# Sparse attention feeding a softplus feed-forward layer: a condition on the strided visits, and a new order for the first chunk

## The chip, the core and the metric

The kernel runs on one core of a Trainium2 chip. Its time is device microseconds of that core. Each core has five engines that run side by side, each through its own list of instructions in order: TensorE (PE, with its weight loads shown as PEld), VectorE (DVE), ScalarE (ACT), GpSimd (POOL) and SyncE (SP), which here issues nearly all DMA transfers. Matmuls write to PSUM, from which ACT and DVE copy results into SBUF.

## What is computed

```python
def attention(q, k, v):                        # 8 batches, 8 heads, 576 positions, 64 wide
    scores = q @ k^T / sqrt(64)
    rel = pos[:, None] - pos[None, :]
    local   = (rel >= 0) & (rel < 32)                       # heads 0 to 3
    strided = (rel >= 0) & (pos[:, None] % 32 == pos[None, :] % 32)   # heads 4 to 7
    scores = where(mask, scores, -1e9)
    return softmax(scores) @ v

x = attention(...)                              # 4608 tokens x 512
h = x @ w_in                                    # 512 -> 2048
g = max(h, 0) + log1p(exp(-|h|))                # softplus
out = g @ w_out                                 # 2048 -> 512
```

All inputs and outputs are float32. For the feed-forward layer the kernel splits every operand into a high and a low part in a format that PE multiplies quickly, and adds three products (high by high, high by low, low by high).

## The kernel before

**Attention.** Two heads make a pair; a batch has two local pairs (0, 1) and two strided ones (2, 3), taken in the order 0, 2, 1, 3, so that the 32 pairs are numbered n = 0 to 31 and every odd n is strided. Pairs 0 to 3 (the first batch) are worked through before the feed-forward layer starts; each later pair n has a *visit* (`visit`, L832), a bundle of small matmuls on PE between two steps of the feed-forward layer. A strided visit first forms the weighted sums of the pair before it (`late_weighted`, L451; its matmuls are L475 or, for a strided pair, L461), then its own scores (`late_scores`, L410; L422 for strided pairs). The strided scores go into two PSUM buffers of the pool `ps_h`, which has just two and is shared with the hidden steps (tile name `ph`). DVE then adds the mask (`add_mask`, L533), and a row softmax follows on DVE and ACT, with DVE transposes at its end (L580 for strided pairs, L592 for local ones).

**Feed-forward layer.** The 4608 tokens are nine chunks of 512, and the 2048 hidden columns sixteen blocks of 128. Step i = 16 x chunk + block. Its hidden part F (`hidden`, L720; twelve matmuls, L729) fills a `ph` buffer. ACT then takes Abs, Exp and Ln (L741, L744, L746), DVE forms the softplus u (`softplus`, L748; the instruction is L750), which sets the `ph` buffer free, and its high and low part. Two steps later the output part O (`output`, L764; twelve matmuls, L769, three for each of four tiles of 128 tokens) adds to the four accumulators `py`. At a chunk's end the `py` banks are copied out (`result`, tile `o`) and stored.

**What sets the order.** Two lists. The first chunk, with the attention of pairs 0 to 8, follows a table of names that is written out by hand (`FIRST`): k, q, v, wi, wo are loads; S scores, X maxima, E exponents, R and M normalization, T transposes, C copies out of PSUM, V weighted sums, H and L the high and low part of x; a, B, d, h, l the conversion of weights; F, A, u, Gh, Gl, O the feed-forward steps; J visits; W filler matmuls. `ON_POOL`, `ON_VECTOR` and `ON_SCALAR` name the steps that leave their usual engine, `WIDE` the two score blocks whose exponents are one wide instruction (after a subtraction on DVE) instead of one for each of their groups. Everything later goes through a planner (`Plan`, L96): each task has an urgency, an engine, a cost and a list of tasks that it stands behind; the planner places them one by one into the first gap of their engine and emits them in the order of planned start. This order becomes the order of each engine's instructions; the waits between engines come from the data. The planner's costs only sort, they don't wait.

A visit S of pair n stands at step i (L1006 to L1009) behind the queries and keys that it needs, the transposes of the pair before, and the softplus of step i - 1. It does not stand behind its own step's softplus u{i}, nor behind the output part O{i-2} that shares its place.

Of the kernel before, what the change touches and what calls it, by code (L numbers as in the profile page):

```python
# [40 lines left out]


FIRST = """
mask k0 q0 wi0 W q1 S01 ai0 X01 k1 S00 wo0 x01 X00 S11 x00 q2 W19 S10 k2 k3 E01 Bi0 q3 E00 X11 di0
ao0 v0 X10 hi0 r0 wi9 x10 R0 M0 S20 T02 Bo0 do0 C02 x11 v1 T00 T01 v2 S21 E10 wi1 X20 li0 E11 C01
C00 S30 ho0 V00 r1 Y20 X21 wi3 R1 x21 E20 S31 v3 V02 E21 Z20 wi2 M1 T11 X30 V01 X31 Y30 H00 q4 r2
C11 R2 L00 lo0 x31 T12 E30 M2 T10 H01 k4 Z30 L01 ai9 C12 E31 V11 T20 C10 Bi9 V12 wo6 V10 r3 T22 C20
H10 di9 T21 R3 L10 wo1 H11 wi4 C22 wo2 L11 M3 V22 C21 ai1 V20 V21 H20 Bi1 di1 T32 hi1 C32 H21 T31
wo3 ai3 L20 C31 L21 Bi3 T30 C30 V32 ai2 di3 li1 V31 V30 H30 H31 hi3 Bi2 wi6 L30 D4 L31 Fa0 di2 wi8
wo4 hi9 ao6 J4 Y42 Y40 v4 hi2 F0 li3 li2 W18 wi10 wi5 ao1 A0 Bo1 Y41 Ae0 Fa1 Al0 wi7 ai4 do1 q5 wo15  # L50
li9 Bo6 F1 wo8 u0 wi13 Gh0 ho1 Km A1 wo10 Bi4 lo1 Ae1 ao3 F2 Gl0 di4 wo5 Al1 hi4 O0 A2 do6 X4 u1 ho6
F3 lo6 ai6 Bi6 Gh1 li4 ao2 Ae2 s4 wo13 Bo2 Al2 Gl1 ai8 di6 Bo3 Bi8 do3 E4 u2 hi6 Z4 r4 do2 k5 ho3
di8 R4 li6 O1 Gh2 A3 Ae3 Al3 M4 F4 u3 Gl2 wi11 P41 ho2 lo2 Gh3 Gl3 F6 O2 A4 wi14 ai5 Ae4 wi12 P40
Al4 lo3 ai7 A6 hi8 P42 Bi5 ao4 Bi7 Kz di5 D5 u4 hi5 Ae6 P43 O3 Al6 u6 Gh4 Gh6 J5 v5 k7 di7 li8 li5
Bo4 ai11 ao5 Y51 wo14 Y50 F5 X5 H40 Gl4 wo7 hi7 Bi11 k6 do4 A5 s5 ho4 E5 Bo5 lo4 li7 Ae5 F9 Z5 ai10
wo11 r5 Al5 wo12 Gl6 di11 R5 wo9 q6 A9 Ae9 Bi10 O4 u5 ao8 di10 M5 do5 Gh5 Al9 hi11 hi10 u9 Gl5 F7
ho5 P53 A7 lo5 F8 H41 Bo8 L40 Ae7 Gh9 P51 ao7 Gl9 wi15 Al7 D6 O5 li10 A8 P50 do8 u7 P52 Ae8 ai12 O6
L41 ho8 Al8 Bo7 J6 u8 li11 v6 F10 Gh7 ai13 Y60 do7 Gh8 H51 Y61 lo8 Gl8 ho7 q7 Y62 X6 Bi12 lo7 H50
Gl7 F11 ao9 A10 di12 s6 ao10 Ae10 hi12 Bi13 Al10 Bo10 di13 u10 A11 O7 li12 E6 ai14 L50 hi13 F12 Z6
r6 Bo9 Ae11 do9 ho9 Bi14 R6 M6 Al11 do10 L51 li13 u11 D7 lo9 O8 Gh11 ho10 F13 ao13 Gh10 P60 Gl11 A12  # L60
O9 P62 di14 P63 Gl10 k8 hi14 Ae12 li14 P61 ao11 A13 Al12 lo10 u12 Ae13 Al13 Gh12 ao12 u13 ai15 Bo11
do11 J7 Bo12 Y71 do12 H61 Y70 O10 X7 Gh13 H60 v7 Gl12 Bo13 ho11 lo11 W23 s7 do13 E7 ho12 Bi15 F14 Z7
r7 A14 lo12 di15 R7 hi15 L61 L60 M7 ao15 li15 Ae14 q8 ho13 D8 P72 Al14 k9 P71 Gl13 lo13 P70 u14 O11
O12 F15 Bo15 A15 O13 P73 Ae15 Al15 J8 Gh14 u15 ao14 Bo14 H70 do14 H71 L71 L70 Qa0 Gl14 q9 Gh15 Q0
do15 ho15 QA0 ho14 lo14 O14 Gl15 Qu0 Q1 lo15 QA1 Ob15 O15 y1 Qu1 Qh0 y2 Qh1 y0 v8 y3 Ql0 Ql1
"""

ON_POOL = """
x00 hi0 r0 x10 x11 x21 x31 r3 hi1 hi9 ho1 hi4 hi8 hi7 r5 hi10 ho5 Gh7 hi13 r6 hi14 ho11 r7 Gh14 ho14
""".split()  # L70
ON_VECTOR = """
M0 C02 li0 C11 C12 C10 C21 C32 li1 hi3 li2 lo1 Gl0 lo6 Gl1 Gl2 Gl4 lo4 Gl6 lo7 Gl7 Gl12 lo12 hi15 D8
Gh15 ho15
""".split()
ON_SCALAR = """
y1 y3
""".split()

WIDE = """
20 30  # L80
""".split()


class Plan:
# [8 lines left out]
    def add(self, name, urgency, engine, cost, fn, after=(), late=0.0):  # L93
        self.tasks[name] = (urgency, len(self.tasks), engine, cost, fn, after, late)

    def run(self):  # L96
        busy, end, start = {}, {}, {}

        def place(name):
            if name in end:  # L100
                return
            _, _, engine, cost, _, after, late = self.tasks[name]
            after = [a for a in after if a in self.tasks]
            for a in after:
                place(a)
            t = max([end[a] + self.WAIT for a in after], default=0.0)
            spans = busy.setdefault(engine, [])
            for x, y in spans:
                if y > t:
                    if x - t >= cost:  # L110
                        break
                    t = y
            spans.append((t, t + cost))
            spans.sort()
            start[name], end[name] = t, t + cost + late

        for name in sorted(self.tasks, key=lambda n: self.tasks[n][:2]):
            place(name)
        for name in sorted(self.tasks, key=lambda n: (start[n], self.tasks[n][1])):
            self.tasks[name][4]()  # L120
# [3 lines left out]
def attention_softplus_ffn(  # L124
# [10 lines left out]
    B, NPAIR, _, _, S = qk.shape  # L135
# [95 lines left out]
    def is_local(n):  # L231
        return order[n][1] < NPAIR // 2
# [38 lines left out]
    def lay_out_q(n, engine=nc.scalar):  # L271

        to = qT[:, :S].rearrange("p (m l) -> p m l", l=32)
        copy_on(engine, to, raws[n].rearrange("p (l m) -> p m l", l=32))
# [535 lines left out]
    LAG = 2  # L810
# [124 lines left out]
    t = 0.0  # L935
# [16 lines left out]
    def visited(i):  # L952
        return when[i] + (2.72 if pushes(i) else 0)

    for i in range(begin, len(steps) + LAG):
        if i < len(steps):
            c, f = steps[i]
            x = when[i]
            after = [f"F{i-1}", f"u{i-2}"] + wanted.get(c, [])
# [173 lines left out]
```

## Time and profile before

| | |
|---|---|
| median of 3 runs | 878.86 us (878.12 to 880.0) |
| the profiled execution | 880.72 us |
| its span, first to last instruction | 878.9 us |
| PE busy | 863.3 us, 98% |
| DVE busy | 590.4 us, 67% |
| ACT busy | 395.5 us, 45% |
| mean granted TensorE clock | 0.998 |

A row of an engine's instructions reads: start, duration, engine, source line, operation, output tile <- input tiles, shapes, how often in a row; in brackets the idle time of the engine ahead of it and what ended it. A row of the list of waits reads: who waited <- for whom: total us, times, longest. A row by stretches gives for each engine its busy time and, in brackets, its number of instructions, then the granted TensorE clock, the share of DMA and GB/s. Matmuls overlap, so each row of PE is longer than its share of the stream; what counts is the distance between starts.

### The profile page before, as it was taken

To read this page: it belongs to the slowest core of one execution; us is meant where nothing else is said; L and a number is where in the kernel's file an instruction comes from. 1 tells how busy PE (TensorE), PEld (TensorE's weight loads), DVE (VectorE), ACT (ScalarE), POOL (GpSimd) and SP (SyncE) were. 2 spreads that over 40 slices of the span, in tenths; PEclk is the share of its full clock that TensorE was granted. 3 is DMA by queue.
4 is the path that set the end of the run, shared out by engine and by line. 5 is a ranking of instruction groups with operands and counts; after the bars stand their busy time and mean duration, and the time that the engine had idled before them with its cause. 6 is when DMAs were issued, how large, how long until landed. Compare 5 with 4: busy or idle time off the path is not lost.

```text
span 878.9 us, 16412 instructions
## 1 busy us (share of the span) xinstructions
PE 863.3 (98%) x6704; PEld 706.5 (80%) x6704; DVE 590.4 (67%) x1282; ACT 395.5 (45%) x703; POOL 75.4 (9%) x97
## 2 busy tenths in 40 slices
PE   7999999999999999999999999999999999999998
PEld 4788888888788878888788878888788888888886
DVE  5999968777876777768685867677776533333332
ACT  5877735444444443443444444344443333333332
POOL 4566650000000000000000000000000000000000
PEclk9999999999999999999999999999999999999999
DMA  9975103111210121102211121012100010001001
GB/s 305 345 274 188 48 14 103 49 50 43 90 42 22 49 75 42 43 28 56 76 43 42 43 90 43 15 47 85 41 16 16 1 48 1 1 1 48 1 1 48
DMA packets 46465, 56.46 MB, mean 64 GB/s; under 512 B 3322, under 2 KB 31670, under 8 KB 46390
## 3 DMA queue, kind: packets, MB, share of 16 engines
q1 hardware_dynamic: 46102, 55.09, 19.5%
q8 instruction: 52, 0.85, 0.4%
q10 hardware_dynamic: 288, 0.33, 0.2%
q14 instruction: 23, 0.19, 0.1%
HBM read 45.97 MB, written 9.44 MB: 63 GB/s over the span
## 4 chain that ended last, share of the span: by engine, by line
PE 95%; ACT 2%; DVE 2%; issue 1%; DMA 1%; SPq 0%; POOL 0%; DVEq 0%; ACTq 0%
PE ph L729 45%; PE py L769 44%; PE ps L422 1%; PE ps L461 1%; PE ps L443 1%; PE ps L475 1%; DMA early_h<-in_qk_dram 1%; DVE u L750 1%; ACT u L744 1%; ACT u L746 1%; ACT u L741 0%; PE pv L622 0%; PE py L393 0%; PE po L443 0%; PE po L461 0%
## 5 line engine op out<-in xcount | busy, mean ns | idle before, releaser
L769 PE MATMUL py<-w_o,gh 128*128 128x512 f32 x1152 | 357.8, 392 | 0.0
L729 PE MATMUL ph<-x_h,w_i 128*128 128x512 f32 x1152 | 355.6, 390 | 1.0 <-DVE prob L533 0.5
L741 ACT ACTIVATE u<-ph 128x512 f32<-128x512 f32 x144 | 86.1, 598 | 376.0 <-PE ph L729 375.7
L729 PEld LDWEIGHTS ph<-x_h,w_i 128*128 128x128 f32 x1152 | 215.6, 188 | 47.0 <-DVE u L750 1.1
L769 PEld LDWEIGHTS py<-w_o,gh 128*128 128x128 f32 x1152 | 214.3, 188 | 44.8
L769 PE MATMUL py<-w_o,gl 128*128 128x512 f32 x576 | 224.2, 389 | 0.0
L729 PE MATMUL ph<-x_l,w_i 128*128 128x512 f32 x576 | 224.1, 389 | 0.0
L750 DVE SCALAR_TENSOR_TENSOR u<-ph,u 128x512 f32<-128x512 f32 x144 | 99.2, 689 | 181.6 <-ACT u L746 180.1
L769 PEld LDWEIGHTS py<-w_o,gl 128*128 128x128 f32 x576 | 108.1, 188 | 22.7
L729 PEld LDWEIGHTS ph<-x_l,w_i 128*128 128x128 f32 x576 | 108.1, 188 | 22.6
L762 DVE TENSOR_TENSOR gl<-u,gh 128x512 fp32r<-128x512 f32 x135 | 93.4, 692 | 10.9 <-PE po L475 0.5
L746 ACT ACTIVATE u<-u 128x512 f32<-128x512 f32 x144 | 91.0, 632 | 4.3
L744 ACT ACTIVATE u<-u 128x512 f32<-128x512 f32 x144 | 91.0, 632 | 4.3
L592 DVE STREAM_TRANSPOSE masks_pt<-prob 32x160 f32<-32x160 f32 x224 | 70.1, 317 | 3.9
L269 DVE CAST gh<-u 128x512 fp32r<-128x512 f32 x129 | 54.6, 424 | 8.6 <-PE py L769 0.5
L580 DVE STREAM_TRANSPOSE pt_groups<-prob 32x192 f32<-32x192 f32 (+1 forms) x112 | 39.6, 354 | 3.1
L580 DVE STREAM_TRANSPOSE masks_pt<-prob 32x160 f32<-32x160 f32 (+1 forms) x112 | 39.6, 354 | 3.1
L548 ACT ACTIVATE prob<-prob 128x576 f32<-128x576 f32 (+1 forms) x28 | 19.4, 693 | 46.2 <-DVE prob L542 46.2
L269 ACT COPY qT<-prob 128x576 f32<-128x576 f32 x27 | 34.5, 1279 | 6.0 <-PE ps L422 5.2
L552 DVE TENSOR_REDUCE st<-prob 128x9 f32<-128x576 f32 (+1 forms) x28 | 21.2, 758 | 9.2 <-ACT prob L548 9.2
L533 DVE TENSOR_TENSOR prob<-ps,masks_pt 128x320 f32<-128x320 f32 (+1 forms) x28 | 10.8, 390 | 24.6 <-PE ps L443 14.5
L269 DVE COPY o<-py 128x512 f32<-128x512 f32 (+1 forms) x16 | 10.7, 670 | 16.9 <-PE py L769 16.9
(105 smaller groups left out, 587.1 us busy)
## 6 DMA issues: line engine op xcount, KB each, us to landing
out_dram<-o SPq DMA_DIRECT2D x35, 256.0 KB, 2.0
ri<-in_moe_w_in_dram SPq DMA_DIRECT2D x16, 512.0 KB, 9.8
ro<-in_moe_w_out_dram SPq DMA_DIRECT2D x16, 512.0 KB, 6.8
prob<-in_qk_dram SPq DMA_DIRECT2D x28, 288.0 KB, 2.8
kT<-in_qk_dram SPq DMA_DIRECT2D x28, 288.0 KB, 3.4
v_in<-in_v_dram SPq DMA_DIRECT2D x14, 162.0 KB
v_in<-in_v_dram SPq DMA_DIRECT2D x14, 160.0 KB, 3.1
v_in<-in_v_dram SPq DMA_DIRECT2D x14, 128.0 KB, 3.1
```

The costliest lines, as they stand in the source:

```text
L269: (engine.copy if engine is nc.scalar else engine.tensor_copy)(dst, src)
L548: nc.scalar.activation(pv, pv, AF.Exp, scale=SCALE)
L552: nc.vector.tensor_reduce(sm, pv, axis=AX.X, op=ALU.add)
L580: nc.vector.transpose(dst[:, :, :32], src[:, :, :32])
L592: nc.vector.transpose(pt_late[lo : lo + 32, h, windows, col : col + 32], src[:, :, 32 * c : 32 * c + 32],)
L729: nc.tensor.matmul(ph, lhsT=w32["i", f][:, half, cc * P : (cc + 1) * P], rhs=x_of(x, cc)[:, t0 : t0 + n], start=(i == 0), stop=(i == 3 * N ...
L741: nc.scalar.activation(us[c, f], phs[c, f], AF.Abs)
L744: nc.scalar.activation(u, u, AF.Exp, scale=-1.0)
L746: nc.scalar.activation(u, u, AF.Ln, bias=1.0)
L750: nc.vector.scalar_tensor_tensor(u, in0=phs.pop((c, f)), scalar=0.0, in1=u, op0=ALU.max, op1=ALU.add)
L762: engine.tensor_tensor(g, us.pop((c, f)), ghs[c, f].bitcast(F32), op=ALU.subtract)
L769: nc.tensor.matmul(py[t], lhsT=g[:, sl], rhs=w32["o", f][:, half], start=(f == 0 and n == 0), stop=(f == NFC - 1 and n == 2),)
```

## The change

Two things change. In the later list a strided visit gets two more tasks that it stands behind: the whole output part of its place, O{i-2}, and its own step's softplus u{i}, the latter with a lead of 0.7 us, by which the planner may place the visit ahead of the softplus' end (a name in the list may now be a pair of a name and a lead). In the first list the names stand in another order, with some steps on other engines and another block among the wide ones.

```diff
@@ FIRST, ON_POOL, ON_VECTOR, WIDE: the tables are replaced; for example
-mask k0 q0 wi0 W q1 S01 ai0 X01 k1 S00 wo0 x01 X00 S11 x00 q2 W19 S10 k2 k3 E01 Bi0 q3 E00 X11 di0
+mask k0 q0 k1 W S01 q1 wi0 S00 q2 k3 X01 x01 k2 X00 S11 E01 wo0 ai0 x00 S10 q3 wi1 E00 X11 X10 v0 v1
...
 WIDE = """
-20 30
+21 30
 """.split()
@@ Plan.run
-            after = [a for a in after if a in self.tasks]
-            for a in after:
+            after = [a if isinstance(a, tuple) else (a, 0.0) for a in after]
+            after = [(a, lead) for a, lead in after if a in self.tasks]
+            for a, _ in after:
                 place(a)
-            t = max([end[a] + self.WAIT for a in after], default=0.0)
+            t = max([end[a] + self.WAIT - lead for a, lead in after], default=0.0)
@@ the visits of the later list
         after += [f"P{n-1}", f"v{n-1}", f"u{i-1}"]
+        if not is_local(n):
+            after += [(f"u{i}", 0.7), f"O{i-LAG}"]
         if n > 2 * NPAIR:
             add(f"S{n}", x, "PE", 1.75, lambda n=n: visit(n), after)
```

**PE at step 34, visit 13 (the third chunk's third hidden part, then the first output part of that chunk).** Here ph_2 is the hidden part, py_108 to py_111 the four output tiles, ps and po the banks of the weighted sums. Before:

```order
L729 MATMUL ph_2_2786<-x_l_591,w_i_659 128x512
L769 MATMUL py_108<-w_o_385,gh_0_2752 128x512 x2
L769 MATMUL py_108<-w_o_385,gl_0_2761 128x512
L475 MATMUL ps_2815<-masks_pt,v_in 64x64 x2
L475 MATMUL po_2816<-masks_pt,v_in 64x64 x2
```

Now:

```order
L731 MATMUL ph_2_2793<-x_l_620,w_i_577 128x512
L771 MATMUL py_108<-w_o_497,gh_0_2759 128x512 x2
L771 MATMUL py_108<-w_o_497,gl_0_2768 128x512
L771 MATMUL py_109<-w_o_497,gh_0_2759 128x512 x2
L771 MATMUL py_109<-w_o_497,gl_0_2768 128x512
L771 MATMUL py_110<-w_o_497,gh_0_2759 128x512 x2
L771 MATMUL py_110<-w_o_497,gl_0_2768 128x512
L771 MATMUL py_111<-w_o_497,gh_0_2759 128x512 x2
L771 MATMUL py_111<-w_o_497,gl_0_2768 128x512
L477 MATMUL ps_2835<-masks_pt,v_in 64x64 x2
L477 MATMUL po_2836<-masks_pt,v_in 64x64 x2
```

Three of the four output tiles have moved ahead of the visit; before, they stood behind its scores. The same happens at visits 17, 21, 25 and 29, the strided visits in the first output step of a chunk. The other strided visits of the later list stood behind a whole output part already, and their place is unchanged.

**DVE at the same place.** ps_0 and ps_1 are the two halves of the strided scores, u_2, gh_2 and gl_2 the softplus of step 34 and its parts. Before:

```order
L750 SCALAR_TENSOR_TENSOR u_2_2811<-ph_2_2786,u_2_2811 128x512
L269 CAST gh_2_2871<-u_2_2811 128x512
L533 TENSOR_TENSOR prob<-ps_0_2837,mask_g 128x324
L762 TENSOR_TENSOR gl_2_2885<-u_2_2811,gh_2_2871 128x512
L533 TENSOR_TENSOR prob<-ps_1_2838,mask_g 128x270
```

Now:

```order
L752 SCALAR_TENSOR_TENSOR u_2_2818<-ph_2_2793,u_2_2818 128x512
L271 CAST gh_2_2881<-u_2_2818 128x512
L764 TENSOR_TENSOR gl_2_2883<-u_2_2818,gh_2_2881 128x512
L535 TENSOR_TENSOR prob<-ps_0_2857,mask_g 128x324
L535 TENSOR_TENSOR prob<-ps_1_2858,mask_g 128x270
```

The low part of g has moved ahead of the first add-mask, which now stands directly ahead of the second.

**ACT in the first list, around the first copy of an attention result.** early_l_94 to early_l_100 hold the probabilities of pairs 0 to 3 (94, 96, 98, 100), st their sums; x_h with pv is the copy of an attention result; masks_pt and early_h_99 receive transposed probabilities out of PSUM (pt). Before:

```order
L503 ACTIVATE early_l_98<-early_l_98 128x6x64
L521 ACTIVATE early_l_98,st_351<-py_109,st_351 128x64 x3
L663 CAST x_h_440<-pv_0_387 128x288
L503 ACTIVATE early_l_100<-early_l_100 128x6x64
L663 CAST x_h_440<-pv_1_388 128x288
L689 ACTIVATE a_i_464<-ri_278 128x512
L521 ACTIVATE early_l_100,st_432<-py_111,st_432 128x64 x3
```

Now:

```order
L523 ACTIVATE early_l_98,st_324<-py_108,st_324 128x64 x6
L691 ACTIVATE a_i_404<-ri_258 128x512
L505 ACTIVATE early_l_98<-early_l_98 128x3x64
L271 COPY masks_pt<-pt_0_399 128x4x96
L271 COPY masks_pt<-pt_2_421 128x4x96
L505 ACTIVATE early_l_100<-early_l_100 128x6x64
L523 ACTIVATE early_l_100,st_412<-py_111,st_412 128x64 x3
L665 CAST x_h_460<-pv_0_430 128x288
```

All exponents of pair 3 (early_l_100) have moved ahead of the first copy of an attention result; pair 2 (early_l_98) has six single exponents where it had one wide instruction.

More of the change, by code (lines that the diff above doesn't have):

```diff
@@ L43 @@
 FIRST = """
-mask k0 q0 wi0 W q1 S01 ai0 X01 k1 S00 wo0 x01 X00 S11 x00 q2 W19 S10 k2 k3 E01 Bi0 q3 E00 X11 di0
[L45 to L63, printed above, removed]
@@ L64 @@
-O12 F15 Bo15 A15 O13 P73 Ae15 Al15 J8 Gh14 u15 ao14 Bo14 H70 do14 H71 L71 L70 Qa0 Gl14 q9 Gh15 Q0
-do15 ho15 QA0 ho14 lo14 O14 Gl15 Qu0 Q1 lo15 QA1 Ob15 O15 y1 Qu1 Qh0 y2 Qh1 y0 v8 y3 Ql0 Ql1
+mask k0 q0 k1 W S01 q1 wi0 S00 q2 k3 X01 x01 k2 X00 S11 E01 wo0 ai0 x00 S10 q3 wi1 E00 X11 X10 v0 v1
+x10 r0 wi3 v2 E10 x11 E11 Bi0 R0 wi2 ao0 M0 W15 S20 X20 T01 S21 di0 x20 E20 v3 S30 wo1 S31 hi0 r1
+T00 C01 ai1 Bo0 R1 X21 Y21 k4 q4 X30 wi4 X31 E21 li0 Y30 C00 T02 Z21 wi6 x31 M1 V00 do0 r2 C02 Bi1
+E30 E31 T11 wi9 V02 R2 Z30 V01 H00 M2 C11 L00 wo2 T10 T12 H01 C10 C12 L01 T21 V10 r3 ai3 wo3 R3 M3
@@ new lines @@
+ho0 Bi3 V12 lo0 C21 V11 H10 L10 T22 H11 wi12 L11 T20 C20 wi8 C22 ai2 V21 V20 V22 T30 H20 T31 W23 W17
+di1 C30 di3 wo6 L20 Bi2 H21 L21 di2 T32 hi3 hi2 V30 C31 C32 V31 hi1 ao1 V32 Bo1 Km li3 Fa0 H30 L30
+H31 L31 D4 li2 v4 do1 J4 li1 Y40 ai4 F0 ho1 Bi4 ai6 A0 Ae0 q5 Fa1 F1 wi10 Al0 Y42 Y41 ai9 X4 di4 lo1
+u0 s4 hi4 Gh0 wi14 A1 Bi9 E4 Bi6 Gl0 F3 Ae1 Al1 O0 di6 di9 hi6 ao3 u1 Kz F2 li4 A3 wo15 ao2 k5 Bo3
+wo13 Ae3 li6 ao6 wo4 wi5 hi9 Gh1 Al3 Gl1 li9 Z4 ai8 u3 Bi8 Bo6 r4 di8 F6 wi7 wo8 A2 Bo2 Ae2 do2 R4
@@ new lines @@
+Al2 O1 M4 do3 u2 W18 wo11 hi8 Gh3 ho3 ho2 Gh2 D5 Gl3 A6 Ae6 wo9 do6 ho6 wo5 Gl2 P43 lo2 wo7 F4 P40
+P42 Al6 A4 ai5 Ae4 lo3 u6 Al4 ai7 P41 u4 li8 Bi7 q6 ai10 lo6 Gh4 Bi5 O2 Gh6 J5 di5 Y50 wo10 hi5 di7
+ao4 li5 Bo4 O3 Y51 X5 hi7 li7 Bi10 s5 F5 do4 E5 wi11 ho4 di10 Gl4 v5 k6 Z5 F9 H41 Gl6 ao7 H40 A5 Bo7
+ao5 Ae5 A9 Al5 lo4 r5 Bo5 ao9 R5 M5 do5 L40 wi15 Ae9 O4 u5 Al9 wo14 L41 do7 F7 ho5 Gh5 u9 ho7 P52
+Gl5 lo5 A7 hi10 Ae7 P53 Gh9 P50 Al7 u7 F8 lo7 Gl9 ai12 wi13 D6 ai11 O5 P51 Gh7 Bo9 Bi11 di11 J6 Y60
@@ new lines @@
+O6 Bi12 do9 A8 Y62 Y61 hi11 li10 ho9 ao8 X6 Bo8 di12 s6 Ae8 hi12 E6 li11 F10 do8 Gl7 O7 Al8 li12 v6
+Z6 u8 r6 ho8 A10 R6 M6 lo8 Gh8 ai13 Ae10 P61 Al10 Gl8 F11 A11 u10 k7 ao10 wo12 Bi13 Ae11 F12 di13
+ai14 lo9 Gh10 W19 O8 hi13 ao11 Gl10 P62 Al11 H50 li13 ai15 P60 u11 A12 Bo10 F13 Ae12 Gh11 q7 k8 D7
+O9 Bi14 H51 Bi15 Al12 Gl11 Bo11 di14 hi14 P63 A13 L51 Ae13 do10 L50 u12 Al13 u13 ho10 lo10 ao12 W21
+do11 J7 ho11 di15 Bo12 Y71 H61 O10 H60 li14 hi15 li15 lo11 ao15 Gh13 do12 v7 Gh12 q8 F14 ho12 Y70
@@ L66 @@
+ao13 X7 Gl12 Gl13 Bo13 F15 s7 do13 E7 O11 A14 Z7 L60 r7 Ae14 ho13 Al14 R7 lo12 A15 u14 L61 M7 Ae15
+ao14 P70 O12 D8 P72 lo13 Al15 P73 Gh14 P71 Bo14 O13 u15 J8 k9 do14 H71 Gl14 Gh15 ho14 L71 H70 Qa0
+lo14 q9 L70 Q0 Bo15 do15 ho15 QA0 Gl15 v8 Qu0 lo15 O14 Q1 Qh0 QA1 Ob15 Qu1 O15 y3 y1 y2 Qh1 y0 Ql1
+Ql0
 """
 ON_POOL = """
-x00 hi0 r0 x10 x11 x21 x31 r3 hi1 hi9 ho1 hi4 hi8 hi7 r5 hi10 ho5 Gh7 hi13 r6 hi14 ho11 r7 Gh14 ho14
+x01 x00 x10 r0 hi0 r1 r3 hi3 hi1 ho1 hi4 hi9 r4 r5 ho5 Gh5 Gh9 r6 ho8 Gh10 hi13 hi14 r7 ho15
@@ L70 @@
 """.split()
 ON_VECTOR = """
-M0 C02 li0 C11 C12 C10 C21 C32 li1 hi3 li2 lo1 Gl0 lo6 Gl1 Gl2 Gl4 lo4 Gl6 lo7 Gl7 Gl12 lo12 hi15 D8
-Gh15 ho15
+M0 C01 C10 M3 ho0 hi2 li2 li1 Gl0 li4 li6 Gh1 li9 li5 Gl4 Gl6 M6 lo9 lo10 lo11 Gl12 Gl13 lo12 ho14
+Gl15 lo15
 """.split()
```

## The prediction

> **What bounds the kernel now.** I read the page first, then busy time by stretches, then the waits, then the order of time around the longest of them. The page:
>
> ```profile
> span 878.9 us, 16412 instructions
> PE 863.3 (98%) x6704; PEld 706.5 (80%) x6704; DVE 590.4 (67%) x1282; ACT 395.5 (45%) x703; POOL 75.4 (9%) x97
> PE 95%; ACT 2%; DVE 2%; issue 1%; DMA 1%; SPq 0%; POOL 0%; DVEq 0%; ACTq 0%
> ```
>
> TensorE (PE) is busy in 98% of the span, and 95% of the chain that ended last is PE. A change can only pay where PE starts its stream earlier, or where it stands still inside it. By stretches (busy us and count of PE, PEld, DVE, ACT, POOL; then granted clock, DMA share, GB/s):
>
> ```profile
> 7.20:30.28 23.08, 18.85 (x392) 13.86 (x384) 17.97 (x43) 17.07 (x69) 8.26 (x14) 0.93 0.99 333
> 30.28:59.26 28.98, 28.87 (x194) 23.10 (x192) 27.69 (x61) 25.99 (x45) 19.57 (x24) 1.00 0.96 342
> 59.26:80.70 21.44, 20.90 (x169) 17.21 (x168) 19.72 (x42) 16.03 (x29) 14.05 (x14) 1.00 0.58 203
> 80.70:98.98 18.28, 18.28 (x190) 15.30 (x190) 17.53 (x39) 13.75 (x24) 11.06 (x11) 1.00 0.17 52
> 98.98:119.83 20.85, 20.85 (x170) 16.94 (x168) 19.50 (x45) 11.65 (x21) 13.50 (x12) 1.00 0.15 44
> ```
>
> PE runs almost without a gap from 30.28 on, where the first hidden matmul stands. Ahead of that it waits for the attention of the first four pairs. From 30.28 to 119.83 DVE is busy 27.69 + 19.72 + 17.53 + 19.50 = 84.44 us of 89.55 (94%): in the first chunk DVE is all but a second bound. Later only one wait of PE is left that repeats:
>
> ```profile
> PE ps L422 <- DVE u L750: 5.3, 5, 1.1
> ```
>
> L422 is the score matmul of a strided visit, L750 the softplus. Five times PE waits 1.1 us for it. One of the five in order of time (visit 13, step 34), and a strided visit that does not wait (visit 15):
>
> ```profile
> 230.80 0.62 PE L769 MATMUL py<-w_o,gh 128*128 128x512 f32 x2
> 231.00 0.60 ACT L741 ACTIVATE u<-ph 128x512 f32<-128x512 f32 x1 [2.55 <-PE ph L729]
> 232.35 0.29 PE L422 MATMUL ps<-kT,qT 64*64 64x54 f32 x4
> 232.96 0.69 DVE L750 SCALAR_TENSOR_TENSOR u<-ph,u 128x512 f32<-128x512 f32 x1 [1.36 <-ACT u L746]
> 233.70 0.80 PE L422 MATMUL ps<-kT,qT 64*64 64x54 f32 x40 [1.06 <-DVE u L750]
> 234.44 0.50 PE L769 MATMUL py<-w_o,gh 128*128 128x512 f32 x1
> ...
> 282.18 0.27 PE L475 MATMUL ps<-masks_pt,v_in 64*64 64x64 f32 x2
> 282.96 0.87 PE L422 MATMUL ps<-kT,qT 64*64 64x54 f32 x44
> 283.76 0.50 PE L769 MATMUL py<-w_o,gh 128*128 128x512 f32 x1
> ```
>
> At visit 13 the scores hold PE from 232.35 to 234.44, 2.09 us; at visit 15 from 282.96 to 283.76, 0.80 us. The difference is **1.29 us**. The reason is read from the first rows: hidden step 34 ends at 230.80, its softplus at 232.96 + 0.69 = 233.65, and only then is the second of the two `ph` buffers free for the scores. One output tile (0.68 us) and the weighted sums are too little work to cover that.
>
> **The later visits.** The change puts visits 13, 17, 21, 25 and 29 behind the whole output step. No instruction is added or removed there; three output tiles of three matmuls move ahead of the visit. A whole step lasts:
>
> ```profile
> 250.37 2.72 PE py L769 x12
> ```
>
> So the weighted sums start at 230.80 + 2.72 + about 0.09 of switching = 233.61, last 282.96 - 282.18 = 0.78 as at visit 15, and the scores start at 234.39, which is 0.74 after the softplus has ended at 233.65. The wait goes whole: 5 x 1.29 = **6.45 us**. What is late next? First, output tiles 1 to 3 stand earlier and need their `py` banks, which the copies of the chunk before set free:
>
> ```profile
> 229.72 0.68 DVE L269 COPY o<-py 128x512 f32<-128x512 f32 x1
> 230.91 0.68 DVE L269 COPY o<-py 128x512 f32<-128x512 f32 x1
> 234.57 0.50 DVE L533 TENSOR_TENSOR prob<-ps,mask_g 128x324 f32<-128x324 f32 x1 [0.46 <-PE ps L422]
> 235.58 0.43 DVE L533 TENSOR_TENSOR prob<-ps,mask_g 128x270 f32<-128x270 f32 x1
> ```
>
> Tile 1 would start at 231.48 (free since 230.40), tile 3 at 232.84 (free since 231.59): over 1 us spare. Second, the scores end at 235.19 instead of 234.44, so the two add-masks (0.50 and 0.43, now side by side) end near 236.2; the next hidden step, which takes their buffer, now has 2.72 us of output ahead of it instead of 4.76 and starts near 238.0: 1.8 us spare. Third, the softmax of pair 13 runs 0.75 us later while PE is 1.29 earlier, and in its stream stands softplus 36, which sets the buffer of hidden step 38 free:
>
> ```profile
> 249.31 0.69 DVE L750 SCALAR_TENSOR_TENSOR u<-ph,u 128x512 f32<-128x512 f32 x1
> 250.03 1.44 DVE L580 STREAM_TRANSPOSE masks_pt<-prob 32x160 f32<-32x160 f32 x4
> 252.93 0.62 PE L729 MATMUL ph<-x_h,w_i 128*128 128x512 f32 x2
> 255.74 0.45 PE L443 MATMUL ps<-kT,qT 64*32 64x64 f32 x32
> ```
>
> 252.93 - 250.00 = 2.93 are spare now, 2.93 - 0.75 - 1.29 = 0.89 remain. The transposes end at 251.47, and visit 14 stands at 255.74, so 4.27 us shrink to 2.2. No new wait follows. If these covers failed, a place would keep up to its whole 1.29: the bounds of this term are 0 and 6.45, and I take 6.45, since visit 15 is this very arrangement and costs 0.80.
>
> **The first chunk.** Its work is the same, with another engine for some steps and another order. First the start of the hidden steps. ACT stands on the path there:
>
> ```profile
> 7.80 0.30 ACT L521 ACTIVATE early_l<-py,st 128x64 f32<-128x64 f32 x1
> 20.86 0.40 ACT L663 CAST x_h<-pv 128x288 fp32r<-128x288 f32 x1 [2.88 <-PE pv L622]
> 23.24 0.31 ACT L521 ACTIVATE early_l<-py,st 128x64 f32<-128x64 f32 x1
> 29.16 0.48 ACT L269 COPY early_h<-pt 128x384 f32<-128x384 f32 x1 [0.18 <-PE pt L604]
> 30.28 0.74 PE L729 MATMUL ph<-x_h,w_i 128*128 128x512 f32 x2
> ```
>
> The last exponents (23.24, three of pair 3) stand behind the first copy of pair 0's result, which idles 2.88 us for PE; from them to the first hidden matmul it takes 7.0 us. The new list puts two copies out of PSUM and all of pair 3's exponents ahead of that copy, so they no longer wait for it. Against that ACT gets more to do. Its groups between 7.2 and 29.7:
>
> ```profile
> L521 ACT ACTIVATE early_l<-py,st 128x64 f32<-128x64 f32 x24 | 7.2, 321 | 0.6 <-POOL st L515 0.6
> L663 ACT CAST x_h<-pv 128x288 fp32r<-128x288 f32 x6 | 2.2, 402 | 4.3 <-PE pv L622 4.3
> L269 ACT COPY masks_pt<-pt 128x384 f32<-128x384 f32 x4 | 1.8, 480 | 0.9 <-PE pt L604 0.9
> L269 ACT CAST w_o<-a_o 128x512 fp32r<-128x512 f32 x1 | 0.6, 632 | 0.0
> L269 ACT COPY early_h<-pt 128x384 f32<-128x384 f32 x2 | 1.0, 485 | 0.2 <-PE pt L604 0.2
> ```
>
> These idle 0.6 + 4.3 + 0.9 + 0.2 = 6.0 us; the other 29.64 - 7.22 - 6.0 = 16.4 us are work. Added: 27 exponents for 24, at 0.29 a piece back to back (0.9), ten copies out of PSUM for six (4 x 0.43 = 1.7 back to back); removed: one cast (0.5). That makes 18.5 us, beginning near 7.5. With no wait at all the last copy ends at 26.0 and the first hidden matmul stands 0.6 behind it, near 26.6: 3.7 earlier. With all 6.0 of today's waits it stands at 32.6: 2.3 later. The 2.88 are filled by the work now ahead of them, and DVE loses four of its six copies out of PSUM here, so I put the waits left at 2.0: start near 28.6, **1.7 us earlier**.
>
> Then that lead has to survive 90 us in which DVE is 94% busy. Summed by the durations that the trace has for each form, DVE's steps up to the last transpose that visit 8 waits for come to some 2 us less in the new order (174 steps for 177: the laying out of visit 8's queries and four copies out of PSUM go to ACT, two normalizations come from POOL). A lead of 1.7 fits that; I keep 1.8 as this term, with bounds of 3.7 gained and, if DVE loses it all again and stalls as below, 2.3 lost. The tail behind the last visit has the same order and adds nothing.
>
> Sum: 6.45 + 1.8 = 8.25 us. The profiled execution took 880.72 around a span of 878.9; the change would bring it to 872.5. The runs' median is 878.86, 1.86 below the profiled one, and no term depends on that, so the forecast is 878.86 - 8.25 = **870.6**.
>
> **Rivals.**
> *The lead is lost in the first chunk.* PE starts earlier and then stands before DVE, as it does today at visit 5:
>
> ```profile
> 60.04 0.87 PE L422 MATMUL ps<-kT,qT 64*64 64x54 f32 x44
> 61.45 0.70 PE L729 MATMUL ph<-x_h,w_i 128*128 128x512 f32 x2 [0.54 <-DVE prob L533]
> ```
>
> For it: 94% busy. Against: 5 us of idle DVE. Only the later term remains: 878.86 - 6.45 = 872.4.
> *The wait moves.* At each of the five places the next hidden step waits for the add-masks, or step 38 for its softplus, and half of the 1.29 comes back: 3.2 + 1.8 gained, 873.8. Against it stand the margins of 1.8 and 0.89. If the wait comes back whole, since the buffer is not what holds the scores, the change there does nothing: 877.1.
> [...]
> *Slower.* DVE is the bound of the first chunk and its new order leaves it idle more. Its 84.44 us at 85% busy instead of 94% last 99.3 instead of 89.55, 9.8 later: 878.86 - 6.45 + 9.8 = 882.2. It decides from 86% down (98.2, +8.6 against 6.45 and the 1.7 of the start). For it: 78% (17.97 of 23.08) ahead of 30.28. Against: behind 30.28 no stretch is under 92%.
>
> **How the numbers follow.** Forecast 0.66 (its own range 868 to 872.3); lead lost 0.15; half of the wait back 0.07; whole back 0.03; cold start 0.05; slower 0.04. The range, 867.8 to 873.6, takes in the lead lost and the cold start, and most of the bounds of the start. A measurement of this kernel tells 0.2% (1.76 us) from no change: faster means below 877.1. All cases but the whole return and the slower one are there: 0.93; within it 0.04, slower 0.03.
>
> **What would show it.** Right: no wait of L422 for the softplus in the list of waits, every strided visit's scores 0.80 us, the hidden step behind them without a gap; first hidden matmul near 28.6, visit 8 near 118. Wrong: a new row PE ph behind DVE prob at five places; a first hidden matmul behind 30.3; DVE under 86% between it and visit 8.

## The result and the profile after

| | before | after |
|---|---|---|
| median, runs of the same batch | 879.35 us (4 runs, 878.12 to 880.0) | 871.76 us (4 runs, 871.48 to 872.58) |
| ratio | | 0.9917, 95% interval 0.9900 to 0.9934 |
| profiled execution | 880.72 us, span 878.9 | 871.48 us, span 869.7 |
| mean granted clock of the profiled execution | 0.998 | 0.999 |

The change takes 7.59 us off the median. The two profiled executions differ by 9.2 us, more than the medians; the last two sections come back to why.

The page of the changed kernel:

```profile
span 869.7 us, 16394 instructions
PE 860.6 (99%) x6708; PEld 705.5 (81%) x6708; DVE 589.6 (68%) x1281; ACT 399.6 (46%) x715; POOL 70.7 (8%) x92
PE 96%; ACT 1%; DMA 1%; POOL 0%; issue 0%; DVE 0%; SPq 0%; DVEq 0%; ACTq 0%
```

The same stretches as before (busy us of PE, PEld, DVE, ACT, POOL, then granted clock, DMA share, GB/s), cut at the first hidden matmul, at visit 5 and visit 6, and at visit 8 (the last row takes in two of the rows before):

```profile
7.20:27.96 20.76, 17.51 (x382) 13.14 (x373) 15.93 (x42) 18.55 (x79) 10.35 (x21) 1.00 1.08 383
27.96:54.44 26.48, 26.12 (x182) 20.86 (x180) 25.51 (x55) 23.26 (x40) 17.52 (x18) 1.00 0.99 363
54.44:75.29 20.85, 20.85 (x169) 17.21 (x169) 20.29 (x44) 15.76 (x29) 14.32 (x13) 1.00 0.52 169
75.29:117.14 41.85, 41.85 (x370) 34.49 (x369) 39.69 (x86) 29.98 (x53) 22.20 (x19) 1.00 0.20 64
```

The first hidden matmul stands at 27.96 and not at 30.28. DVE is busy 25.51 + 20.29 + 39.69 = 85.49 of the 89.18 us behind it, 96%. The stretch from visit 5 to visit 6 took PE 20.90 busy in 21.44 us before; it is 20.85 in 20.85 now, without a gap. The head's granted clock is 1.00, where before had 0.93.

PE's list of waits, its first rows:

```profile
PE py L377 <- ACT early_l L523: 1.3, 1, 1.3
PE idle L794 <- DVE room L219: 1.2, 1, 1.2
PE pv L624 <- POOL early_l L566: 0.8, 1, 0.8
PE pv L624 <- DVE x_l L663: 0.5, 2, 0.3
```

The row of five waits for the softplus, 5.3 us, is gone, and nothing took its place: these rows lie in the head, ahead of the first hidden step, and behind it the list has one wait left, of 0.2 us. Visit 13 in order of time (L424 are the scores, L752 the softplus, L535 the add-masks):

```profile
230.14 0.69 DVE L752 SCALAR_TENSOR_TENSOR u<-ph,u 128x512 f32<-128x512 f32 x1 [1.40 <-ACT u L748]
231.57 0.87 PE L424 MATMUL ps<-kT,qT 64*64 64x54 f32 x44
232.37 0.73 PE L771 MATMUL py<-w_o,gh 128*128 128x512 f32 x2
232.47 0.84 DVE L535 TENSOR_TENSOR prob<-ps,mask_g 128x324 f32<-128x324 f32 x2 [0.46 <-PE ps L424]
```

The softplus ends at 230.14 + 0.69 = 230.83, the scores start at 231.57, and the next matmul follows them 0.80 us later, as at visit 15 of the kernel before.

### The profile page after: what moved, and what is told of

It reads as the page before. It is cut to its first block, busy times and chain, and to the rows that moved or that the text cites. A ratio compares the mean times of both kernels' runs of the same rounds, so it can differ in the third digit from the quotient of the medians.

```text
span 869.7 us, 16394 instructions
## 1 busy us (share of the span) xinstructions
PE 860.6 (99%) x6708; PEld 705.5 (81%) x6708; DVE 589.6 (68%) x1281; ACT 399.6 (46%) x715; POOL 70.7 (8%) x92
## 4 chain that ended last, share of the span: by engine, by line
PE 96%; ACT 1%; DMA 1%; POOL 0%; issue 0%; DVE 0%; SPq 0%; DVEq 0%; ACTq 0%
PE py L771 45%; PE ph L731 45%; PE ps L477 1%; PE ps L424 1%; PE ps L463 1%; PE ps L445 1%; DMA ri<-in_moe_w_in_dram 1%; ACT early_l L523 1%; PE pv L624 0%; PE pt L606 0%; PE po L445 0%; PE po L463 0%; PE po L477 0%; ACT x_h L665 0%; POOL w_i L717 0%
## 5 line engine op out<-in xcount | busy, mean ns | idle before, releaser
L752 DVE SCALAR_TENSOR_TENSOR u<-ph,u 128x512 f32<-128x512 f32 x144 | 99.1, 688 | 182.8 <-ACT u L748 181.5
L582 DVE STREAM_TRANSPOSE pt_groups<-prob 32x160 f32<-32x160 f32 (+1 forms) x112 | 39.6, 354 | 3.0
L665 ACT CAST x_h<-ps 128x288 fp32r<-128x288 f32 (+5 forms) x34 | 11.8, 365 | 24.5 <-PE po L477 20.1
L535 DVE TENSOR_TENSOR prob<-ps,masks_pt 128x320 f32<-128x320 f32 (+1 forms) x28 | 10.8, 389 | 17.3 <-ACT x_h L665 9.9
```

Source lines behind the costliest of these rows:

```text
L582: nc.vector.transpose(dst[:, :, :32], src[:, :, :32])
L752: nc.vector.scalar_tensor_tensor(u, in0=phs.pop((c, f)), scalar=0.0, in1=u, op0=ALU.max, op1=ALU.add)
```

## The experiments

**The rule without the new list, and the new list without the rule.** The first kernel has the change's condition on strided visits and the old tables of the first chunk; the second has the new tables and the old condition.

```diff
 rule_only:  after, with the tables FIRST, ON_POOL, ON_VECTOR, WIDE of before
 order_only: before, with the tables FIRST, ON_POOL, ON_VECTOR, WIDE of after
```

> Edit: the old tables, with the new condition on the strided visits. If the five waits of 1.29 us are the later part and the two parts of the change add up, this is 6.45 us faster than before (872.9 of 879.35), its first hidden matmul stays near 30.3, every strided visit's scores take 0.80 us from visit 13 on, and the wait of visit 5 in the first chunk (0.54) stays. If the new order were needed for the later gain (its earlier start leaving DVE more room), some of the waits would remain and less than 6.45 comes.

> Edit: the new tables, without the new condition. The profiled executions of before and of the change differ by 2.8 us at visit 9 (first hidden matmul 30.28 against 27.96, the rest at visit 5), the medians leave only 7.59 - 6.45 = 1.1 us for this part. If the new order starts the hidden steps 2.3 us earlier in every execution, this is 2 to 2.8 us faster than before (876.5 to 877.4 of 879.35); if the profiled execution of before was a long one in its first 30 us and the order itself gives little, about 1.1 us or less (878.2). The five waits of 1.06 us must all be there again.

Measured: the rule alone 873.63 us (872.67 to 874.38, 5 runs) against 879.66 (15 runs), ratio 0.9937 (0.9924 to 0.9949), 6.03 us less. The list alone 877.90 (877.75 to 879.09, 11 runs), ratio 0.9982 (0.9973 to 0.9991), 1.76 less. 6.03 + 1.76 = 7.79, and the whole change measured 7.59: the parts add. With the list alone the five waits are back in the same size:

```profile
PE ps L423 <- DVE u L751: 5.3, 5, 1.1
```

With the rule alone they are gone, and the smaller wait behind visit 5, where a hidden step needs the score buffer that the add-mask still holds, is still there:

```profile
29.60 0.72 PE L730 MATMUL ph<-x_h,w_i 128*128 128x512 f32 x2
59.35 0.87 PE L423 MATMUL ps<-kT,qT 64*64 64x54 f32 x44
60.76 0.70 PE L730 MATMUL ph<-x_h,w_i 128*128 128x512 f32 x2 [0.54 <-DVE prob L534]
```

So the later visits are the rule's, and visit 5 is the list's.

**How far behind must the visit stand?** The rule's two conditions do not weigh the same: with O{i-2} alone the planner emits the very order of the change, so u{i} adds nothing beside it; with u{i} alone it puts the visit behind three of the four output tiles. Two kernels put it behind a fixed number of tiles:

```diff
         if not is_local(n):
-            after += [(f"u{i}", 0.7), f"O{i-LAG}"]
+            after += [f"O{i-LAG}.1"]      # two_tiles;  three_tiles: f"O{i-LAG}.2"
```

> Edit: the new kernel, but a strided visit in the first output step of a chunk stands behind two of the four output tiles instead of all four. If the scores wait for a PSUM buffer that the softplus of the same step sets free at a fixed time after its hidden part, each tile ahead of the visit covers 0.68 us of it: from 2.09 us with one tile the scores fall to 1.41, so the five places cost 5 x 0.61 = 3.05 us more than the new kernel (874.8 of 871.76), with a wait of PE for the softplus of about 0.4 us at each. If the wait hung on something that comes with the whole output step (its last tile, the copies of the banks), it would stay at 2.09 (878.2).

> Edit: as before with three of four tiles ahead of the visit. By the fixed time the wait is covered with 0.06 us to spare: the scores take 0.80 to 0.85 and the time is that of the new kernel, within 0.3 us. By the other reading the wait stays at 2.09 us or close to it (878.2). With this the condition on the softplus alone can be judged too, since it puts the visit at this very place.

Measured: two tiles 874.75 (874.35 to 874.95, 4 runs), ratio 0.9949 (0.9936 to 0.9963); three tiles 871.60 (871.35 to 871.76, 4 runs), ratio 0.9914 (0.9900 to 0.9927). The scores of visit 13 with two tiles, and then with three:

```profile
230.98 0.80 PE L424 MATMUL ps<-kT,qT 64*64 64x54 f32 x40 [0.39 <-DVE u L752]
```

```profile
230.99 0.87 PE L424 MATMUL ps<-kT,qT 64*64 64x54 f32 x44
```

With two tiles PE waits 0.39 us for the softplus and the scores take 1.41; with three they do not wait. Each tile put ahead takes its 0.68 us from the wait of 1.06 until nothing is left. The fourth tile buys nothing: three and four tiles differ by 0.16 us, within what the runs scatter.

**The reason given for the head.** The prediction had ACT on the path: pair 3's exponents stood behind a copy that idled for 2.88 us. This kernel makes that move alone:

```diff
-... X31 Y30 H00 q4 r2 / C11 R2 L00 lo0 x31 T12 E30 M2 T10 H01 ... C12 E31 V11 ...
+... X31 Y30 x31 E30 E31 H00 q4 r2 / C11 R2 L00 lo0 T12 M2 T10 H01 ... C12 V11 ...
```

> The kernel before with one move in the first list, the one on which my head term rests: pair 3's offsets and exponents (x31, E30, E31) go ahead of the first copy of an attention result on ACT (H00). No other part of the change. Theory (ACT's chain sets the first hidden-layer matmul; the first copy waits 2.88 us for PE while pair 3's exponents, 1.1 us of work, stand behind it): the first hidden-layer matmul comes 1 to 1.7 us earlier than in the kernel before (30.28 us in a profile with the low clock, about 29.2 without), median 878.0-878.6. Rival (another resource closes the gap: DVE's list, PE's own work or the inputs from memory): the first hidden-layer matmul moves by less than 0.4 us, median 879.2-880.

Measured: 879.41 (878.82 to 880.97, 12 runs) against 879.47 (23 runs), ratio 1.0005 (0.9996 to 1.0013). The kernel before was profiled once more for comparison:

> The kernel before, unchanged, profiled once more: its first profile fell in an execution whose granted clock went to 0.50 for some 3.5 us. If that alone makes the long executions, a profile with a clock of 1.00 throughout has its first hidden-layer matmul about 1.0 us earlier than 30.28 us, that is near 29.2, and a span near 877.5; the wait at visit 5 (0.61 us) and the five waits of 1.29 us stay. If the profile falls in a low-clock execution again, it shows 30.3 and 879 again and says only that the two agree.

It took 878.74 with a span of 877.0 and a granted clock of 1.0. Its copy of the first result and its first hidden matmul:

```profile
19.12 0.40 ACT L663 CAST x_h<-pv 128x288 fp32r<-128x288 f32 x1 [1.55 <-PE pv L622]
28.36 0.74 PE L729 MATMUL ph<-x_h,w_i 128*128 128x512 f32 x2
```

and those of the kernel with the exponents moved, also at full clock there:

```profile
18.98 0.52 ACT L503 ACTIVATE early_l<-early_l 128x384 f32<-128x384 f32 x1 [1.16 <-DVE early_l L498]
20.28 0.40 ACT L663 CAST x_h<-pv 128x288 fp32r<-128x288 f32 x1
29.02 0.73 PE L729 MATMUL ph<-x_h,w_i 128*128 128x512 f32 x2
```

At full clock the copy idles 1.55 us and not 2.88: the rest of that idle time came in the first profile with TensorE near half its clock (granted 0.63 from 15.20 to 17.20 us and 0.52 from 17.20 to 19.20, against 1.00 in the second). And the moved exponents do not fill it. They wait 1.16 us for a subtraction on DVE, push the copy from 19.12 to 20.28, and the first hidden matmul comes 0.66 us later, not earlier: one engine's idle time was filled with work that another engine had not yet made ready. This alone leaves open whether the move would pay with the subtraction done in time. The changed kernel answers that, for there the exponents don't wait. The last of pair 3's exponents, in the second profile of the kernel before and then in the changed kernel:

```profile
21.89 0.33 ACT L521 ACTIVATE early_l<-py,st 128x64 f32<-128x64 f32 x1
```

```profile
18.29 0.45 ACT L523 ACTIVATE early_l<-py,st 128x64 f32<-128x64 f32 x1
```

They end at 18.74 and not at 22.22, 3.5 us earlier, and the first hidden matmul comes only 0.40 us earlier, at 27.96. So these exponents do not set the start of the hidden steps.

**The granted clock in the head.** The first profile of the kernel before shows the clock near half for a while (0.52 from 17.20 to 19.20 us); the second does not (1.00). Is it because PE idles there, and can dummy matmuls prevent it? Three kernels: before with eight more dummies in PE's gaps, after with six more, and after without its three pairs.

```diff
 before_warm: -X00 S11 x00 q2         +X00 W30 S11 x00 q2
              -x11 v1 T00 T01 v2      +x11 v1 W31 W32 T00 W33 T01 v2
 after_warm:  -M0 W15 S20             +M0 W15 W30 W31 S20
              -C00 T02 Z21            +C00 T02 W32 Z21
 no_fillers:  W15, W23 and W17 are left out of FIRST
```

> The kernel before with eight more small dummy matmuls (0.26 us each in the profiles) on PE, put where PE stands idle in the first 16 us: two behind the first two projected pairs, six around the first transposes (12.7 to 14.9 us in the profile of before). Nothing else is changed, the result of the dummies is not used. Theory A (the granted clock falls to 0.5 for some 3.4 us in part of the executions because PE is idle too often just before, and such an execution is about 1.0 us longer): the executions with a mean granted clock of 0.998 become rare, the median falls from about 879.6 to 878.4-878.9. Rival B (the clock falls whatever PE does, by the moment at which the program starts): as many executions at 0.998 as before, the median stays at 879.4-880. Rival C (the dummies push back the real work that they stand ahead of): 880 or more, with the first hidden-layer matmul later than 30.28 us.

> The changed kernel with six more of the same dummy matmuls: four in the 1.26 us in which PE waits for ACT at 9.7 to 11.0 us, two behind a transpose at about 17 us. Theory A (as in before_warm: idle PE makes the clock fall): no execution at a mean clock of 0.998, median 871.4-871.8, the slowest execution below 872.2. Rival B (chance of the start): about one execution in four is at 0.998 and lasts some 872.6, median unchanged. Rival C (delay): median 872 or more with every clock at 1.0.

> The changed kernel without its three pairs of dummy matmuls in the first list behind the opening burst (the first at 9.4 us, ahead of the idle 1.26 us; two later ones at about 24-27 us). Theory A (idle PE makes the clock fall): more than half of the executions have a mean clock of 0.998 or less, median up by 0.7 to 1.2 us to 872.3-872.9. Rival B (chance): one in four at 0.998 as before, median 871.3-871.9; it may even be 0.2-0.5 faster, if the dummies held real work up.

Measured: before_warm 880.68 (878.64 to 881.26, 11 runs), ratio 1.0012 (1.0002 to 1.0021), with a mean clock of 0.998 in 6 of 11 executions; after_warm 871.78 (871.49 to 872.03, 4 runs), ratio 0.9915 (0.9901 to 0.9928), 0 of 4; no_fillers 871.19 (870.76 to 872.54, 4 runs), ratio 0.9911 (0.9896 to 0.9925), two of 4 below 0.998. The theory that idle PE alone brings the low clock is not borne out for the kernel before: with eight dummies it has the low clock as often as without (11 of 23 beside it), and is a little slower for them. The clock does not explain that: three of its five executions at 0.999 or 1.0 took 880.33 to 880.68, and its first hidden matmul, profiled at full clock, stands at 28.42 against 28.36. In the changed kernel the counts run the way the theory has it: 0 of 4 with six more dummies, 1 of 4 in the change itself, 2 of 4 without the three pairs. Four runs each are too few to tell this from chance. By the medians, neither more nor fewer dummies make a difference there that four runs can tell. Among executions at 0.999 or 1.0 the kernel without them is 0.9 us faster (870.78, mean of two, against 871.67, mean of three), so they may cost time and keep the clock up; that is not shown.

**An output step behind the visit instead of ahead of it.** Visit 5's wait of 0.54 us is gone with the new list, in which the output step O3 follows the visit. This kernel makes that swap in the old list, with visit 5's data made ready earlier:

```diff
-P42 Bi5 ao4 Bi7 Kz di5 D5 u4 hi5 Ae6 P43 O3 Al6 u6 Gh4 Gh6 J5 v5
+P42 P43 u4 Bi5 ao4 Bi7 Kz di5 D5 hi5 Ae6 Al6 u6 Gh4 Gh6 J5 O3 v5
```

> The kernel before with one move in the first list, at visit 5: the output step O3 goes behind the visit (as the new list has it) in place of ahead of it, and pair 4's last transposes and hidden step 4's softplus go ahead of the random-number work on DVE so that the visit finds its data. Theory: the hidden step behind the visit no longer waits for the mask add on the score buffer (0.61 us between first hidden step and visit 6 in the profile of before), median 0.4 to 0.7 lower, 878.7-879.0 against 879.4. Rival: the visit, now 2.7 us earlier, waits for its transposes or for a free score buffer instead, 879.3-880, and the 0.61 us are found again at the visit's own matmuls.

Measured: 885.42 (883.87 to 886.81, 6 runs), ratio 1.0071 (1.0057 to 1.0085): some 6.5 us slower than the 878.97 beside it, outside both expectations, though the rival named the kind of wait. PE and DVE at the visit:

```profile
56.49 0.29 PE L422 MATMUL ps<-kT,qT 64*64 64x54 f32 x4
57.43 0.68 DVE L700 SCALAR_TENSOR_TENSOR a_i<-ri,a_i 128x512 uint32<-128x512 uint32 x1
60.06 0.69 DVE L750 SCALAR_TENSOR_TENSOR u<-ph,u 128x512 f32<-128x512 f32 x1 [1.95 <-ACT u L746]
60.80 1.33 PE L422 MATMUL ps<-kT,qT 64*64 64x54 f32 x40 [4.03 <-DVE u L750]
```

and ACT:

```profile
58.15 0.62 ACT L269 CAST w_i<-a_i 128x512 fp32r<-128x512 f32 x1 [2.66 <-DVE a_i L700]
58.67 0.62 ACT L744 ACTIVATE u<-u 128x512 f32<-128x512 f32 x1
```

It is the wait of visits 13 to 29 once more, nearly four times as long: the second score buffer is held by hidden step 6 until its softplus at 60.06. An output step (O2) does stand between the two, but my own edit made the softplus late. With the transposes and softplus 4 ahead, the work on DVE that stood behind them ends at 57.43 + 0.68 = 58.11 (the expectation calls it random-number work; by the kernel it is the conversion of the weights, which arrive as 64-bit numbers, by a shift and a combining of their two words); a cast of weights on ACT waits 2.66 us for it; and the last two steps of softplus 6 stand behind that cast on ACT. Then the clock pays on top (granted clock is the third number from the end):

```profile
58.00:60.00 2.00, 0.00 (x0) 0.00 (x0) 0.11 (x1) 1.82 (x4) 1.16 (x1) 0.86 0.48 142
60.00:62.00 2.00, 1.20 (x40) 1.16 (x40) 1.63 (x3) 1.63 (x4) 0.70 (x2) 0.50 0.00 0
62.00:64.00 2.00, 2.00 (x13) 1.55 (x6) 1.80 (x4) 0.90 (x3) 1.44 (x2) 0.50 0.33 56
64.00:66.00 2.00, 2.00 (x6) 1.59 (x5) 2.00 (x5) 0.00 (x0) 0.00 (x0) 0.50 1.01 374
66.00:68.00 2.00, 2.00 (x9) 1.61 (x8) 0.38 (x2) 0.00 (x0) 0.00 (x0) 0.93 0.99 359
```

So this run does not give the value of the swap. What it shows is how near the place is to its limit: in the changed kernel the same softplus ends 0.20 us before the scores start (54.33 + 0.69 = 55.02, and 55.22).

```profile
54.33 0.69 DVE L752 SCALAR_TENSOR_TENSOR u<-ph,u 128x512 f32<-128x512 f32 x1 [0.56 <-ACT u L748]
55.22 0.87 PE L424 MATMUL ps<-kT,qT 64*64 64x54 f32 x44
```

**Visit 8's add-masks.** In the changed kernel two starts of PE's blocks between 121 and 131 us were late by 0.32 and 0.18 us. Visit 8's mask adds stand on DVE behind the softplus of hidden steps 16 and 17, though DVE idles ahead of both:

```profile
121.66 0.69 DVE L764 TENSOR_TENSOR gl<-u,gh 128x512 fp32r<-128x512 f32 x1
124.01 0.69 DVE L752 SCALAR_TENSOR_TENSOR u<-ph,u 128x512 f32<-128x512 f32 x1 [1.67 <-ACT u L748]
129.79 0.69 DVE L752 SCALAR_TENSOR_TENSOR u<-ph,u 128x512 f32<-128x512 f32 x1 [4.15 <-ACT u L748]
132.26 0.68 DVE L535 TENSOR_TENSOR prob<-ps,masks_pt 128x320 f32<-128x320 f32 x2
```

```diff
-... QA0 Gl15 v8 Qu0 ...
+... QA0 Gl15 Y80 Y81 Y82 v8 Qu0 ...      (and the planner no longer adds them for pair 8)
```

> The changed kernel with one more move: visit 8's three mask adds go into the first list directly behind the last chunk-0 low part, where DVE stands idle for 1.67 us from 122.35, in place of behind the softplus of hidden steps 16 and 17 at 132.26. They free the score buffer that the hidden steps wait for. Theory: the small waits in 121-131 us (0.32 and 0.18 us) go, median 871.0-871.4 against 871.7. Rival: the waits are for the softplus of those steps itself and stay: 871.6-872.

> The changed kernel with both: visit 8's mask adds early, as in mask8, and without the three pairs of dummy matmuls, as in no_fillers. If the two add: 870.3-870.9 (no_fillers measured 871.19, mask8 takes 0.3-0.5 from it). If no_fillers' lower median was chance: as mask8, 871.0-871.5, with more executions at a clock below 0.999.

Measured: mask8 870.78 (870.64 to 871.88, 4 runs) against 878.97 (11 runs), ratio 0.9908 (0.9894 to 0.9923); with the dummies left out too 870.38 (869.73 to 871.28, 4 runs), ratio 0.9900 (0.9888 to 0.9913). The adds moved into the idle time:

```profile
122.22 0.68 DVE L535 TENSOR_TENSOR prob<-ps,masks_pt 128x320 f32<-128x320 f32 x2
122.82 0.28 DVE L535 TENSOR_TENSOR prob<-po,masks_pt 128x128 f32<-128x128 f32 x1
123.97 0.69 DVE L752 SCALAR_TENSOR_TENSOR u<-ph,u 128x512 f32<-128x512 f32 x1 [0.87 <-ACT u L748]
```

From visit 8 to visit 9 PE now takes 146.26 - 117.10 = 29.16 us; in the changed kernel it takes 147.10 - 117.14 = 29.96. That 0.80 is seen in the trace and is more than the 0.32 + 0.18 that the theory counted. Both late starts are gone there, so the rival, a wait for the softplus itself, falls. The medians agree with it, while the intervals of the three kernels overlap. Without the dummies the executions at 0.999 or 1.0 are again faster, 870.16 against 870.73 (means of three), but that rests on few executions too. The last kernel is the fastest measured here, by its median 1.4 us below the change.

## Why the prediction was right, and where it was not

**The later visits, 6.45 us: right.** Every step of that working stands in the trace after. The margin between the end of the softplus and the scores was predicted as 0.74 us and is 231.57 - 230.83 = 0.74. All five places went from 2.09 to 0.80 us. The rule alone took 6.03 off the median; compared between executions of equal clock it is 880.31 - 873.84 = 6.47 (means of eight and four executions at 0.998 or below); at a higher clock there is one execution of it, 878.91 - 872.67 = 6.24. The covers named for what is late next held: no wait of a hidden step for add-masks or for softplus 38 came up. "The wait moves" is refuted, and "the buffer is not what holds the scores" too, by the kernels with two and three tiles. (The half return, 873.8, was counted inside the range 867.8 to 873.6 and lies just outside it.)

**The first chunk, 1.8 us: the amount fits, the working does not.** The list alone measured 1.76, which looks like a hit. It is made of other things, and the hit is luck.

- *The start, "1.7 us earlier, near 28.6": the step that failed.* It compared with a first hidden matmul at 30.28, which belonged to an execution with a low clock in the head. The prediction saw that this execution took 1.86 us more than the runs' median and held that no term depended on it; this term did. At full clock the kernel before starts at 28.36 and the changed one at 27.96: 0.40 earlier. Of the 1.92 us between the two starts of the kernel before, 0.42 was there ahead of the fall of the clock: the copy that waits for the transposes starts on ACT at 14.87 in the second profile and at 15.29 in the first, where an early matmul had waited 0.78 us for a load and not 0.3. The cause named, pair 3's exponents on ACT's path, does not hold either: alone they cost 0.66 us, and 3.5 us earlier in the changed kernel they go with only 0.40. The count of ACT's work did come out (18.55 us busy and 2.21 idle from 7.20 to 27.96, against 18.5 and 2.0), but it does not set the start. What among the moved names brings the 0.40 was not isolated.
- *"That lead has to survive": it did, and grew a little.* From the first hidden matmul to visit 9 it took 147.95 - 28.36 = 119.59 at full clock, and takes 147.10 - 27.96 = 119.14: 0.45 less. The wait behind visit 5 (0.61 by the starts) is in it, less what other places lose. The prediction had shown that wait as today's example of PE standing before DVE and had not counted its end as a gain. So at equal clock the list is worth 0.40 + 0.45 = 0.85 us. The timed executions at a mean clock of 0.999 or 1.0 are close to it: 878.91 before (mean of 7), 877.95 with the list alone (mean of 9), 0.96 apart. One term of this working was mis-sized beside that: DVE's work was said to shrink by some 2 us, and from 7.20 us to visit 8 it is 0.8 us less (102.21 in the second profile of the kernel before, 101.42 now).
- *The rest of the 1.76* is in part that the low clock is rarer with the new list: in 2 of 11 executions of that kernel, in 8 of 15 of the kernel before beside it. With 1.4 us for each low-clock execution (last section) that is (0.53 - 0.18) x 1.4 = 0.5, and 0.85 + 0.5 = 1.35. The means differ by 1.51. The medians differ by more, since that of the kernel before falls among its low-clock executions and that of the list alone among the others. Whether the list makes the low clock rarer or the few executions fell so was not tested. The cold start, 0.05 of the forecast, stood for a low clock in the head that the new list would bring; that was an estimate, and no run shows it. What the runs show is a low clock in part of the executions of both kernels (23 of 49 of the kernel before, 1 of 4 of the changed one), and the kernel before had it in the very profile that the sum was made on.

**The slower rival.** DVE at 85% would have cost 9.8 us; it is 96% busy between the first hidden matmul and visit 8.

**The sum.** The forecast was 870.6, a gain of 8.25; measured were 871.76 and 7.59, nearer to the rival in which the lead is lost (872.4), though there was little lead to lose. At equal clock 6.45 + 0.85 = 7.30; the two profiled executions at full clock differ by 878.74 - 871.48 = 7.26, and the means of the timed executions at 0.999 or 1.0 by 878.75 - 871.67 = 7.08 (26 and three executions). The medians' 7.59 has a few tenths from the clock on top, and the 9.2 between the first two profiles has a whole low-clock execution.

## What to carry to other kernels

A matmul that needs a shared accumulation buffer belongs behind enough independent matmuls to cover the buffer's last reader, and the distance can be read off in matmul tiles: here 0.68 us of cover for each tile, and two more tiles for a wait of 1.06 us. The cover has to be counted against the reader's whole chain, with what stands ahead of it on each engine: one cast on ACT ahead of a softplus, itself late for DVE, made a wait of 4.03 us. Before an idle stretch of an engine is taken for a gain, look up whether the work to be put there has its inputs by then, and profile the kernel before twice: a head that differs by 1.9 us between two executions of the same program is no base for a term of that size. When the bound engine has only small stalls left, look for a buffer that is held by work queued behind unrelated work on an idle engine: visit 8's add-masks were worth 0.8 us in the trace.

## What the hardware showed beside that

In part of the executions the granted TensorE clock falls to half for about 3.4 us within the first 20 us. The kernel before in its first profile, and the same program in the second one:

```profile
13.20:15.20 2.00, 0.98 (x8) 0.45 (x6) 2.00 (x6) 1.37 (x10) 0.00 (x0) 1.00 1.11 358
15.20:17.20 2.00, 2.00 (x57) 1.41 (x60) 1.03 (x5) 1.91 (x6) 0.62 (x2) 0.63 1.03 301
17.20:19.20 2.00, 2.00 (x57) 1.55 (x49) 1.04 (x2) 0.78 (x6) 1.94 (x2) 0.52 0.97 283
```

```profile
13.20:15.20 2.00, 1.07 (x18) 0.68 (x22) 2.00 (x5) 1.25 (x8) 0.00 (x0) 1.00 1.12 358
15.20:17.20 2.00, 2.00 (x84) 1.56 (x76) 0.99 (x5) 2.00 (x9) 1.14 (x2) 1.00 1.13 354
17.20:19.20 2.00, 1.87 (x41) 1.32 (x39) 1.84 (x6) 0.45 (x4) 1.66 (x3) 1.00 1.08 366
```

The missing clock of the first is (0.37 + 0.48) x 2 = 1.70 us, which is 3.4 us at half; the rows of rule_only, (0.09 + 0.50 + 0.26) x 2 from 13.20 to 19.20 us, and of order_only, 0.08 x 21.20 from 7.20 to 28.40, give the same 1.70, that of mask8_no_fillers, 0.13 x 12.80 from 7.20 to 20.00, gives 1.66. Over the three batches the kernel before was run 49 times: 26 executions at a mean clock of 0.999 or 1.0 took 878.75 us in the mean, 23 at 0.998 took 880.18, so one such fall is worth 1.4 us. All six kernels with the new list and its dummies together have a mean clock of 0.998 or below in 4 of 31, the two without the dummies in 3 of 8.

What sets off the fall in a half-busy head stays open. From 11.20 to 15.20 us, ahead of it, PE was busy 1.53 + 0.98 of 4.00 us in the first profile of the kernel before, and almost the same 1.56 + 1.07 went without a fall in the second. Eight dummies in the gaps of that head did not prevent it (6 of 11 executions). In visit5 a fall came in a stall: PE stood still for 4.03 us, and the clock fell some 2.7 us into that (near 59.45). There it stayed at half for (0.14 + 3 x 0.50 + 0.07) x 2 x 2 = 6.8 us, and PE stood still in about the first 1.3 us of them (the five rows of visit5 from 58 to 68 us that are under 1.00 by 0.14, 0.50 three times, and 0.07).

Twelve matmuls of 128x512 in the format of the high and low parts took 2.72 us in the kernel before, 0.227 us each. No run multiplies unsplit operands, so what that format saves is not shown.
